# Hedgehog attention and spectral mix on one core: v loads on the software queue, permuted last sums with one store a pair, and a reordered tail

## The chip, the cores and the metric

The kernel runs on one core of one Trainium2 chip. The metric is the device time of one execution in microseconds (us), and the kernel before takes 462.76 us (median of three runs, 461.85 to 463.92).

The engines are called PE (matmul), PEld (its weight load), DVE (VectorE), ACT (ScalarE), POOL (GpSimd) and SP (SyncE). A DMA that SyncE issues goes to the hardware queue, q1 in the profile. One that GpSimd issues goes to the software queue, q0, and in this kernel all transfers that turn f32 into bf16 are issued there. The profile counts both queues against the same 16 DMA engines of the core. SBUF is the on-chip memory of 128 partitions that holds the tiles; PSUM is the one into which PE writes its sums.

## The reference

```python
batch, n_heads, seq, head_dim, d_feat = 8, 8, 576, 64, 128
def phi(x):                                   # x: q or k
    proj = einsum('bhsd,df->bhsf', x, w_phi)
    proj -= max(abs(proj), axis=-1)
    return concat([exp(proj), exp(-proj)], axis=-1)
num = q_p @ (k_p^T v);  den = q_p . sum_s(k_p) + 1e-6
x = (num / den) laid out as [8, 576, 512]     # attention output

X = rfft(x, axis=1)                           # 64 modes are used
Yr = Xr @ w_r[m] - Xi @ w_i[m]                # w_r, w_i: [64, 512, 512] f32
Yi = Xr @ w_i[m] + Xi @ w_r[m]
y = irfft(Y, n=576, axis=1)
u = x + y
return u + relu(u @ w_ch)                     # [8, 576, 512] f32, 9.44 MB
```

The two weight arrays are 134 MB of f32, so the kernel has to read 164 MB in all. That is most of its time.

## The kernel before

The work has three stages. In stage 1 attention runs and the weights stream in; each weight tile is read as f32 and lands as bf16. `mix` multiplies a tile with the spectrum. Eight modes make one group `o`, and a finished group is put into `yall` (for x) and, after a product with `w_ch`, into `zall` (for the relu argument). In stage 2, after the last weight tile, the last group goes through a chain: sum, transposes, copy, product, copy. In stage 3 the inverse transform of the last modes is added and the output is stored. The inverse transform of modes 0 to 47 is done earlier, in 36 "absorbs", one for each chunk of 128 rows; three of the 36 come in the last chain.

The loads (v has rows of 9 x 64 f32, which are 2304 bytes):

```python
def load(t, src, g, bp, eng):
    eng.dma_start(t.rearrange("p b c d -> p b (c d)"),
        src[2*bp:2*bp+2, 2*g:2*g+2].rearrange("b h (p c) d -> (h p) b (c d)", c=9))

def load_k(self): ...; load(self.kb, k, self.g, self.bp, pool)   # f32 -> bf16
def load_v(self): ...; load(self.vn, v, self.g, self.bp, sp)     # f32
```

The chain behind the last weight, with the absorbs in it:

```python
mix(*key, wts.pop(key), XTb[g % 2], bank)
...
dve.tensor_tensor(out=yst, in0=py, in1=yacc[:, o, :], op=ALU.add)
put(yst, o, yall, (0, 2))                # two small SyncE copies into yl
if end:
    ab[-3].sums(); ab[-3].keep_x()
for dc in range(4):
    pe.transpose(pt[:, dc, :], yst[:, dc*128:(dc+1)*128], ident_b)
act.copy(yT, pt)
if end:
    ab[-2].sums(); ab[-2].keep_x(); ab[-3].keep_w()
for dc in range(4):
    pe.matmul(pz, lhsT=yT[:, dc, :], rhs=wchb[:, dc, :], ...)
act.copy(zst, pz)
put(zst, o, zall, (1, 3))
if end:
    ab[-2].keep_w(); ab[-1].all()
```

The last sums. A chunk `n` has 128 rows: partition 64*a + p holds row 9*p + 4*a + c of a sequence, so the two halves `a` of the partitions go to two places of the output, and a pair of chunks is stored as two transfers of 64 partitions with 4 KB rows:

```python
class Last:
    def base(self, which):  # starts the PSUM sum: identity times the row so far
        ...
        pe.matmul(self.q[a], lhsT=ident_b, rhs=xw[:, self.bp, n, :], start=True, stop=False)
    def late(self, which): ...      # adds modes 48..63, table CL, from yl
    def straight(self, which): ...  # or the last group from yst / zst, table CM (first chunks)
    def relu(self): ...             # ACT: rl = relu(q)
    def store(self):
        ...
        dve.tensor_tensor(out=o, in0=self.pp, in1=self.rl, op=ALU.add)
        i, c = n // 4, n % 4
        for a in range(2):
            (sp, pool)[a].dma_start(
                rows[i][:, 4*a + c:4*a + c + 2, :], o[64*a:64*a + 64])   # 256 KB each
```

## Time and profile before

| | us, from the trace of the kernel before |
|---|---|
| stage 1: start to the last mix | 416.4 |
| stage 2: last mix to first store issued | 9.9 |
| stage 3: first store to end of the last DVE sum | 25.5 |
| end of the last sum to end of the span | 8.5 |
| span | 460.2 |

These lines are from the page of the kernel before: the DMA row gives the busy share of the 16 DMA engines in tenths, for 40 slices of 11.5 us; the GB/s row what they delivered; the queue lines give packets, MB, and the time of the packets as a share of the 16 engines' span; the last two give KB of one transfer and us from issue to landing.

```profile
span 460.2 us, 9716 instructions
...
DMA  8999999999999999999999999999999999992897
GB/s 192 207 216 220 230 229 209 228 229 207 229 230 209 228 229 227 209 230 229 207 229 228 207 207 207 206 208 207 207 213 218 214 211 211 205 178 55 249 323 252
DMA packets 86301, 99.27 MB, mean 216 GB/s; under 512 B 2800, under 2 KB 79728, under 8 KB 86256
...
q1 hardware_dynamic: 8992, 16.85, 12.0%
...
vn<-in_v_dram SPq DMA_DIRECT2D x16, 576.0 KB, 7.8
...
out_dram<-of SPq DMA_DIRECT2D x16, 256.0 KB, 4.9
```

The reader sees a full DMA row up to the 36th slice, then one slice at 55 GB/s, which is stage 2, then the output. A slice that carries weights alone shows 207 GB/s, because a weight is counted as the bf16 that lands; the f32 read is twice that, 414 GB/s.

This is the timeline of stage 2 in the kernel before: start us, duration, engine, operation, out<-in, count, and in brackets the idle time ahead of it and what ended that.

```profile
416.42 0.67 PE L37 MATMUL pt<-wt,XT 128*32 128x512 bf16 x8 [1.67 <-DMA wt<-in_moe_w_i_dram]
417.13 0.69 DVE L37 TENSOR_TENSOR yst<-pt,yacc 128x512 bf16<-128x512 f32 x1 [2.09 <-PE pt L37]
...
418.37 0.58 ACT L37 COPY yT<-pt 128x512 bf16<-128x512 bf16 x1 [2.94 <-PE pt L37]
...
419.01 1.04 PE L37 MATMUL pt<-wchb,yT 128*128 128x512 bf16 x3
...
420.13 0.58 ACT L37 CAST zst<-pt 128x512 bf16<-128x512 f32 x1 [0.68 <-ACT xw L37]
...
423.06 1.09 ACT L37 ACTIVATE rl<-qq 128x512 f32<-128x512 f32 x2 [1.37 <-PE qq L37]
...
425.01 1.23 DVE L37 TENSOR_TENSOR of<-pp,rl 128x1024 f32<-128x1024 f32 x1 [3.90 <-PE pp L37]
...
426.27 0.53 SPq L37 DMA_DIRECT2D out_dram<-of  x1
```

`zst` is ready at 420.71, yet its first use by the last sums is the matmul whose relu starts at 423.06, and the first output sum waits for the other half of its sum until 425.01. PE works on the remaining absorbs and on the base sums of a whole pair in between.

This is the table by stretch of time of the kernel before; its header line names the columns (busy us and count of each engine, the granted PE clock, the DMA share, GB/s).

```profile
core 0: us, PE busy (x) PEld busy (x) DVE busy (x) ACT busy (x) POOL busy (x), PEclk, DMA share, GB/s
416.00:426.00 10.00, 8.72 (x48) 3.09 (x48) 3.66 (x5) 4.55 (x9) 0.00 (x0) 1.00 0.22 54
428.00:444.00 16.00, 16.00 (x92) 4.81 (x88) 13.60 (x13) 11.56 (x21) 6.36 (x12) 1.00 0.95 312
444.00:452.00 8.00, 6.51 (x38) 1.94 (x36) 6.61 (x7) 4.94 (x9) 3.17 (x6) 1.00 0.94 305
452.00:458.00 6.00, 0.00 (x0) 0.00 (x0) 0.00 (x0) 0.00 (x0) 0.54 (x1) 0.62 0.95 310
```

In the output stage the DMA engines are 94 to 95% busy at only 305 to 312 GB/s, and after the last sum (452) they have six more microseconds of backlog. While v is being loaded the reading rate is also a bit lower: these are the queue lines of the DMA view of the kernel before from 251 to 253 us.

```profile
q1 hardware_dynamic: 174, 0.40, 57.3%
q0 software_dynamic: 173, 0.18, 51.4%
```

The weights' 0.18 MB are 0.36 MB of f32, so 0.76 MB are read in 2 us, 380 GB/s against the 414 of weights alone.

### The profile page before, as it was taken

What the parts mean: (1) busy time and instruction counts of PE and PEld (TensorE: products, weight loads), DVE (VectorE), ACT (ScalarE), POOL (GpSimd) and SP (SyncE); (2) the same over time, 40 slices, a digit from 0 to 9 for tenths busy, and PEclk for the clock granted to TensorE, in tenths of its full rate; (3) what the DMA queues carried; (4) which work ended last, traced back from release to release, by engine and by line L of the source; (5) the groups of instructions that cost most, each with busy time, mean ns of one, the idle gap of its engine ahead of it and who ended that gap; (6) DMA issues with size and microseconds to landing.
All of it is one profiled execution on the core that took longest, in us unless ns stands there. A gap on an engine that the chain in (4) does not pass through costs nothing.

```text
span 460.2 us, 9716 instructions
## 1 busy us (share of the span) xinstructions
PE 331.6 (72%) x4041; PEld 207.1 (45%) x4084; DVE 270.0 (59%) x488; ACT 281.6 (61%) x475; POOL 92.4 (20%) x130
## 2 busy tenths in 40 slices
PE   1586767768767767877866776059997756997991
PEld 1365546546555545655654554024443322332330
DVE  6656676556677658568647784643331213773882
ACT  3696879676889769579758762214452322664771
POOL 6232112113111211222110115002121210000331
PEclk9998999797999999789879999559998987999997
DMA  8999999999999999999999999999999999992897
GB/s 192 207 216 220 230 229 209 228 229 207 229 230 209 228 229 227 209 230 229 207 229 228 207 207 207 206 208 207 207 213 218 214 211 211 205 178 55 249 323 252
DMA packets 86301, 99.27 MB, mean 216 GB/s; under 512 B 2800, under 2 KB 79728, under 8 KB 86256
## 3 DMA queue, kind: packets, MB, share of 16 engines
q0 software_dynamic: 77264, 81.80, 103.8%
q1 hardware_dynamic: 8992, 16.85, 12.0%
q8 instruction: 32, 0.52, 0.4%
q14 instruction: 13, 0.11, 0.1%
HBM read 163.64 MB, written 9.44 MB: 376 GB/s over the span
## 4 chain that ended last, share of the span: by engine, by line
issue 27%; PE 23%; ACT 15%; DMA 15%; DVE 13%; POOL 5%; POOLq 0%; ACTq 0%
PE one L37 9%; PE pt L37 8%; DMA wt<-in_moe_w_i_dram 7%; PE two L37 6%; DVE m L37 6%; DMA kb<-in_k_dram 6%; ACT AB L37 5%; ACT AQ L37 5%; DVE mk L37 2%; POOL wt L37 2%; POOL out_dram L37 2%; DMA qb<-in_q_dram 2%; DVE zall L37 2%; ACT kT L37 2%; ACT XT L37 1%
## 5 line engine op out<-in xcount | busy, mean ns | idle before, releaser
L37 ACT CAST xw<-pt 128x512 bf16<-128x512 f32 x72 | 42.0, 586 | 61.7 <-PE pt L37 60.5
L37 ACT ACTIVATE AB<-two 128x1024 bf16<-128x1024 f32 x64 | 62.8, 1051 | 6.2 <-DVE mk L37 3.8
L37 ACT ACTIVATE AQ<-two 128x1024 bf16<-128x1024 f32 x64 | 63.0, 1053 | 1.9 <-PE two L37 1.8
L37 PE MATMUL pt<-wchb,xT 128*128 128x512 bf16 x135 | 39.8, 412 | 20.0 <-DVE xT L37 19.7
L37 DVE TENSOR_REDUCE m<-two 128x8 f32<-128x1024 f32 x32 | 39.2, 1224 | 17.8 <-PE two L37 17.7
L37 DVE TENSOR_REDUCE mk<-two 128x8 f32<-128x1024 f32 x32 | 39.0, 1221 | 16.7 <-PE two L37 16.3
L37 POOL DMA_DIRECT2D wt<-in_moe_w_r_dram x30 | 26.3, 878 | 95.7 <-PE one L37 52.9
L37 POOL DMA_DIRECT2D wt<-in_moe_w_i_dram x28 | 24.5, 876 | 91.0 <-PE pt L37 46.1
L37 DVE TENSOR_TENSOR va<-vn,ee 128x1152 bf16<-128x1152 f32 x32 | 42.0, 1356 | 0.0
L37 DVE RECIPROCAL rd<-one 128x6 f32<-128x6 f32 x48 | 9.4, 195 | 51.5 <-PE one L37 51.5
L37 ACT COPY kT<-one 128x512 bf16<-128x512 bf16 (+1 forms) x32 | 19.2, 640 | 28.7 <-PE one L37 28.7
L37 DVE TENSOR_TENSOR xs<-pt,xs 128x512 bf16<-128x512 f32 x36 | 24.3, 691 | 19.0 <-PE pt L37 18.6
L37 PEld LDWEIGHTS <-minus 96*128 96x128 bf16 x288 | 26.3, 110 | 19.0 <-issue 13.4
L37 PEld LDWEIGHTS <-XT 128*32 128x32 bf16 x512 | 17.9, 180 | 34.2 <-issue 21.6
L37 PE MATMUL two<-w2blk,qT 128*128 128x256 bf16 x128 | 20.4, 285 | 17.6 <-ACT AB L37 12.9
L37 DVE COPY xT<-pt 128x512 bf16<-128x512 bf16 x36 | 15.1, 422 | 30.3 <-PE pt L37 30.3
L37 PE MATMUL two<-mT,minus 96*128 96x128 bf16 x256 | 29.3, 245 | 3.1 <-issue 1.9
L37 PEld LDWEIGHTS <-xs 128*128 128x128 bf16 x304 | 24.7, 100 | 15.2 <-issue 8.1
L37 POOL DMA_DIRECT2D kb<-in_k_dram x16 | 11.5, 716 | 95.5 <-PE one L37 94.7
L37 PEld LDWEIGHTS <-qT 128*128 128x128 bf16 x144 | 14.1, 101 | 32.5 <-issue 29.9
L37 PE MATMUL one<-kvz,AQ 128*128 128x65 bf16 x512 | 28.0, 211 | 0.0
L37 DVE TENSOR_TENSOR xs<-one,rd 128x384 bf16<-128x384 f32 x48 | 26.8, 558 | 1.6
(113 smaller groups left out, 673.9 us busy)
## 6 DMA issues: line engine op xcount, KB each, us to landing
wt<-in_moe_w_r_dram POOLq DMA_DIRECT2D x30, 1024.0 KB, 28.1
wt<-in_moe_w_i_dram POOLq DMA_DIRECT2D x28, 1024.0 KB, 28.6
vn<-in_v_dram SPq DMA_DIRECT2D x16, 576.0 KB, 7.8
kb<-in_k_dram POOLq DMA_DIRECT2D x16, 288.0 KB, 22.3
qb<-in_q_dram POOLq DMA_DIRECT2D x16, 288.0 KB, 22.1
out_dram<-of SPq DMA_DIRECT2D x16, 256.0 KB, 4.9
out_dram<-of POOLq DMA_DIRECT2D x16, 256.0 KB, 5.0
xs<-in_moe_w_i_dram POOLq DMA_DIRECT2D x2, 1024.0 KB, 26.9
```

What stands on the lines that cost most here:

```text
L37: ins = f(*args, **kwargs)
```

## The change

There are three intents. The v loads go to the software queue, with all other large loads. The output pairs are to be stored by one transfer over all 128 partitions: a permutation matrix takes the identity's place in the last sums and the tables' columns are permuted alike, so that partition 2*p + a holds what partition 64*a + p held. And the tail is reordered: all 36 absorbs come ahead of the last mix; the products of the last three chunks are held in PSUM; the sum, the transposes, the copies and the product of the last group are split into halves of 256 columns, and of the copies ACT takes one half and DVE the other; and the first pair is split into two single chunks, of which the first has its sums started ahead of the last term. The diff also joins the stores of the ninth rows of two batch pairs into one, puts half of the last small copies into `yl` on GpSimd's queue, and drops the separate PSUM pools of the last sums. `K` is 33, so `ab[K:]` are the last three chunks.

```diff
-            load(self.vn, v, self.g, self.bp, sp)
+            load(self.vn, v, self.g, self.bp, pool)
...
+    perm = CF.rearrange("p c r m -> p (c r m)")[:, 512:640]
+    dve.tensor_copy(perm.rearrange("k (p a) -> k a p", a=2),
+                    ident_b.rearrange("k (a p) -> k a p", a=2))
...  (the columns of CL and CM are written in the same order)
+        def hold(self, pf):          # product of a chunk, left open in PSUM
+            for g in range(NG):
+                pe.matmul(pf, lhsT=self.xT[:, g, :], rhs=wchb[:, g, :],
+                          start=(g == 0), stop=False)
...
-    todo += [c.all for c in ab[:-3]]
+    todo += [c.only_x for c in ab[K:]] + [c.only_w for c in ab[K:]] + [c.all for c in ab[:K]]
...
+        if not mixq:                 # ahead of the last mix
+            seq[0].base(1)
+            seq[0].late(1)
         mix(*key, wts.pop(key), XTb[g % 2], bank)
...
+            if end:
+                seq[0].base(0)
+                seq[0].late(0)
...  (yst, yT, zst in two halves of 256 columns; of the copies to yT and zst one half on ACT, one on DVE)
-            if end:
-                ab[-3].sums()
-                ab[-3].keep_x()
...  (likewise ab[-2], ab[-1])
+            elif end:
+                seq[0].straight(0)
+                seq[0].keep_p()
+                seq[1].base(1)
...
+                turned = perm if n < 8 else ident_b
-            for a in range(2):
-                (sp, pool)[a].dma_start(
-                    rows[i][:, 4 * a + c:4 * a + c + 2, :], o[64 * a:64 * a + 64])
+            sp.dma_start(
+                bass.AP(tensor=rows.tensor, offset=rows.offset + n % 4 * DMODEL,
+                        ap=[[9 * DMODEL, 64], [4 * DMODEL, 2], [1, w * DMODEL]]),
+                o.rearrange("p a e -> p (a e)") if w > 1 else o)
...
+    seq = [Last((0, 0)), Last((0, 1))] + [Last(*x) for x in pairs[0][1:] + pairs[1]]
+    seq += [Last((0, 8), (1, 8))] + [Last(*x) for x in pairs[2]] + [Last((2, 8), (3, 8))]
+    seq += [Last(*x) for x in pairs[3]]
```

## The prediction

> **What bounds it now.** Three stages follow one another. (1) Up to 416 us, weight loading. The DMA row is full from 5 to 410 us; the software queue delivers 207 GB/s of bf16, so reads 413 GB/s of f32 (page and per-queue window view). The last mix starts at 416.42, after 1.67 us of waiting for its weight (timeline); PE's absorbs had just fitted. (2) 416.4 to 426.3: a latency chain (sum 0.69, transposes 0.40, copy 0.58, product 1.04, copy 0.58 us) with three absorbs in its way, then the first output pair; DMA share 0.4 (stage table). (3) Output: 9.44 MB from 426.3 to 459. The first output sum starts at 425.0, the last ends at 451.7; PE needs 1.29 us a pair, DVE 1.28. The DMA share is 0.9 to 1.0 at only 300 to 350 GB/s, SyncE's late issues are stretched to 1.7 us, and stores are issued until 455: the DMA is the limit there, compute close behind.
>
> **Costs.** *v on the software queue*: the same bytes. The Trainium skill (DMA: Bandwidth & Descriptors, Issuing engines are not separate DMA queues) says that all issuers share 16 engines, so no bandwidth by itself. But while v flows, the two queues' packets make up 370 to 390 GB/s of reading, against 413 otherwise (1 us windows, 250 to 253): 0.2 to 0.25 us lost a load, 16 loads, at most 4 us. I credit 1.5 us. v lands after about 25 us instead of 7.8, against some 30 us of lead: it just fits, with rare DVE waits that DMA backlog hides.
> *Reordering*: three absorbs (2 us of PE) leave the final chain, three held products fill the idle PE at 377 to 384, halves shorten the chain, and the first chunk needs only its last term. I estimate the first store 4.6 us after the last weight, instead of 9.85: 5 us, all on the critical path. Chunk four's sums then wait shortly (0 to 1 us) for the last small copies (3.4 us landing before). After that 16 steps at about 1.3 us: last store about 30 us after the weight, against 35.3 for the last DVE sum (and 38.5 for SyncE's last issue) before.
> *Stores*: 40 become 19, so completion packets go from 640 to 304. Stores used 466 engine-us; at 25.8 GB/s an engine (the loads' rate) data is 366, leaving 0.156 us a completion packet. Estimate after: 413 engine-us, 25.8 us instead of 29.1, so the stores keep up nearly. The skill (SBUF, Door 1) says that 64 partitions reach half the ports, about 218 GB/s; this trace shows 290 GB/s from SyncE's 64-partition stores alone (456 to 457), so I count little for the full 128. One queue is enough: SyncE issues in 0.6 us when not pushed back.
>
> **Sum.** 462.8 less 1.5 (v), 5.2 (first store), about 3 (drain after compute: 8.5 us becomes 5.5) = 453.0 us; range 449 to 457.5. Chances: faster 0.54, same 0.45, slower 0.01.
>
> **What would show it.** Last mix at 414 to 416.5 us; first store within 5 us of it; DVE output sums 1.3 us apart; under-512 B packets down by 336; output at 360 to 400 GB/s; last store issue near 445; span near 450.5. The v step is right if reading stays above 405 GB/s while v flows; wrong if DVE waits on v leave the DMA row with holes.
>
> **What would make it wrong.** Stores on one queue stuck at 320 to 330 GB/s (455 or more); v late enough to starve the weights; PE, now with 36 absorbs before the last mix and only four single banks, reaching it after the weight; or, to the good, an evener finish of the 16 engines, whose rates fell off unevenly from 410 to 416 (up to 3 us), or v recovering all 4 us.

## The result, and the profile after

The changed kernel takes 452.34 us (median of four runs, 451.45 to 452.55), against 462.54 of four runs of the kernel before. The ratio is 0.9772 (95% interval 0.9745 to 0.9799), so it is faster by 2.3%. A ratio here and below is the mean time of one kernel's runs over that of the other's in the same rounds, so it is not quite the ratio of the medians that are quoted. The kernel before ran on the same chip, so kernels are compared by these ratios.

The two traces add up as follows. Each row is one stage, and the last column is what the changed kernel gains in it.

| us | before | after | gained |
|---|---|---|---|
| last mix starts | 416.42 | 414.26 | 2.16 |
| last mix to first store | 9.85 | 5.15 | 4.70 |
| first store to end of the last sum | 25.45 | 26.32 | -0.87 |
| end of the last sum to end of span | 8.48 | 4.67 | 3.81 |
| span | 460.2 | 450.4 | 9.8 |

This is one profile of each. In the repeat after_again the four stages are 413.25, 5.17, 26.31 and 4.77 us, so the first row is uncertain by about 1 us, and the others repeat within 0.1.

These are the lines of the page of the changed kernel that answer to those shown above, with the group of DVE that reads v (busy us, mean ns, then idle time ahead of it and what ended that).

```profile
span 450.4 us, 9754 instructions
...
DMA  8999999999999999999999999999999999995597
GB/s 162 233 207 207 234 208 234 232 208 261 207 207 234 234 234 232 213 230 227 217 230 225 229 218 206 206 207 207 209 207 220 214 215 214 202 201 100 195 380 314
DMA packets 83981, 99.27 MB, mean 220 GB/s; under 512 B 2464, under 2 KB 79136, under 8 KB 83936
...
q1 hardware_dynamic: 5744, 11.86, 8.1%
...
L37 DVE TENSOR_TENSOR va<-vn,ee 128x1152 bf16<-128x1152 f32 x32 | 42.0, 1355 | 3.4 <-DMA vn<-in_v_dram 3.4
...
vn<-in_v_dram POOLq DMA_DIRECT2D x16, 576.0 KB, 18.4
out_dram<-of SPq DMA_DIRECT2D x17, 512.0 KB, 3.6
```

A v load now takes 18.4 us to land instead of 7.8, and DVE waited for v for 3.4 us in all. The DMA row has no hole while v flows, so those waits cost nothing (v_first2_sp below agrees). Packets under 512 B fell by 336, as predicted. A store of 512 KB lands in 3.6 us, where one of 256 KB took 4.9.

The timeline of the changed kernel, from the last mix to the first store, with the columns of before:

```profile
414.26 0.67 PE L37 MATMUL pt<-wt,XT 128*32 128x512 bf16 x8 [1.43 <-DMA wt<-in_moe_w_i_dram]
...
414.98 0.76 DVE L37 TENSOR_TENSOR yst<-pt,yacc 128x256 bf16<-128x256 f32 x2 [2.25 <-PE pt L37]
...
416.34 1.04 PE L37 MATMUL pt<-wchb,yT 128*128 128x256 bf16 x8
...
417.20 0.37 ACT L37 CAST zst<-pt 128x256 bf16<-128x256 f32 x1 [0.28 <-PE pt L37]
...
418.69 0.69 DVE L37 SCALAR_TENSOR_TENSOR ofr<-pp,rl 128x512 f32<-128x512 f32 x1 [0.80 <-PE pp L37]
...
419.41 0.61 SPq L37 DMA_DIRECT2D out_dram<-ofr  x1
```

The product starts 2.08 us after the last mix (2.59 before), the first output sum 4.43 us after it (8.59 before). `zst` is whole 3.64 us after it (its DVE half ends at 417.90), against 4.29 before. So of the 4.70 us by which the first store comes earlier, 0.65 are gained up to `zst`, 3.51 between `zst` and the first output sum, where the sums of a single chunk now stand ready and no absorb is in the way, and 0.54 in an output sum of half the size. This is read from the two traces; no run took the halves or the split of the first pair away alone. The table by stretch of the changed kernel, with the columns of before:

```profile
414.00:419.00 5.00, 4.68 (x30) 2.19 (x31) 1.78 (x5) 1.33 (x3) 1.05 (x2) 1.00 0.21 52
...
428.00:444.00 16.00, 15.86 (x99) 4.98 (x97) 13.85 (x12) 12.36 (x24) 0.00 (x0) 1.00 0.95 372
444.00:448.00 4.00, 0.25 (x2) 0.00 (x0) 1.72 (x2) 0.47 (x1) 0.00 (x0) 0.89 1.02 406
```

The same busy share of the DMA engines, 0.95, now carries 372 GB/s instead of 312, and 406 from 444 us on, as the last sums end. PE is busy for nearly all of 428 to 444 in both kernels.

### The profile page after: what moved, and what is told of

It reads as the page before. It is cut to its first block, busy times and chain, and to the rows that moved or that the text cites. A ratio compares the mean times of both kernels' runs of the same rounds, so it can differ in the third digit from the quotient of the medians.

```text
span 450.4 us, 9754 instructions
## 1 busy us (share of the span) xinstructions
PE 329.1 (73%) x4069; PEld 209.5 (47%) x4113; DVE 276.3 (61%) x519; ACT 274.6 (61%) x472; POOL 94.8 (21%) x128
## 3 DMA queue, kind: packets, MB, share of 16 engines
HBM read 163.64 MB, written 9.44 MB: 384 GB/s over the span
## 4 chain that ended last, share of the span: by engine, by line
DMA 28%; PE 26%; issue 17%; ACT 12%; DVE 12%; POOL 5%; ACTq 0%; POOLq 0%; DVEq 0%
DMA wt<-in_moe_w_i_dram 13%; PE pt L37 11%; PE one L37 8%; DMA wt<-in_moe_w_r_dram 8%; DMA vn<-in_v_dram 6%; ACT AB L37 5%; PE two L37 4%; DVE m L37 3%; POOL wt L37 3%; ACT AQ L37 3%; PE pp L37 3%; DVE mk L37 2%; DVE zall L37 2%; DVE va L37 1%; DVE xs L37 1%
## 5 line engine op out<-in xcount | busy, mean ns | idle before, releaser
L37 ACT CAST xw<-pt 128x512 bf16<-128x512 f32 x50 | 29.4, 588 | 43.2 <-PE pt L37 43.2
L37 PE MATMUL pt<-wchb,xT 128*128 128x512 bf16 x127 | 36.3, 398 | 22.4 <-DVE xT L37 20.8
L37 PE MATMUL two<-w2blk,qT 128*128 128x256 bf16 x128 | 21.9, 299 | 16.5 <-ACT AB L37 12.3
L37 PEld LDWEIGHTS <-xT 128*128 128x128 bf16 x144 | 13.4, 102 | 32.0 <-DVE xT L37 20.5
L37 PE MATMUL pt<-wt,XT 128*32 128x512 bf16 x208 | 18.5, 431 | 11.4 <-DMA wt<-in_moe_w_i_dram 8.7
L37 PE MATMUL one<-kvz,AQ 128*128 128x65 bf16 x512 | 26.6, 206 | 0.1
## 6 DMA issues: line engine op xcount, KB each, us to landing
vn<-in_v_dram POOLq DMA_DIRECT2D x16, 576.0 KB, 18.4
```

What stands on the lines that cost most here:

```text
L37: ins = f(*args, **kwargs)
```

## The experiments

Twelve kernels ran; ten of them compute the right result. The questions were three. Why do the v loads gain more than the 1.5 us that the prediction gave them? Is the faster output due to fewer completion packets (called C1), as the prediction had it, or to the 128 partitions of a transfer, that is to more ports of SBUF (C2)? And does the reordering gain its time by taking the absorbs out of the chain? A run's first store and last sum are times in its trace.

| kernel | median us (range, runs) | ratio to before | first store | last sum ends | span |
|---|---|---|---|---|---|
| v_only | 458.46 (458.21-458.94, 6) | 0.9938 | 423.35 | 448.80 | 456.5 |
| no_v | 454.28 (453.67-455.12, 4) | 0.9846 | 422.84 | 449.15 | 453.3 |
| split_halves | 460.45 (457.47-463.16, 6) | 0.9981 | 421.58 | 451.16 | 461.4 |
| no_reorder | 455.61 (455.34-456.00, 4) | 0.9875 | 423.38 | 448.98 | 454.2 |
| absorbs_early | 463.46 (460.53-464.78, 6) | 1.0032 | 427.58 | 453.04 | 460.9 |
| split_cols | 454.61 (453.73-458.65, 6) | 0.9867 | 418.99 | 445.30 | 451.9 |
| after_again | 451.98 (451.33-452.27, 4) | 0.9782 | 418.42 | 444.73 | 449.5 |
| halves_warm | 457.88 (457.09-459.46, 6) | 0.9917 | 418.35 | 444.67 | 455.5 |
| absorbs_warm | 461.46 (460.59-461.86, 5) | 0.9988 | 426.30 | 451.75 | 459.7 |
| v_first2_sp | 451.62 (451.42-452.93, 5) | 0.9784 | 418.42 | 444.72 | 449.8 |

The kernel before had medians of 461.23, 461.49 and 461.78 us in the three calls (11 runs each). The 95% intervals of the ratios are within 0.0034 of them. The two kernels that compute nothing, micro_stores and micro_loads, ran once each and are read by their traces alone.

### v_only: the kernel before with v on the software queue

```diff
-            load(self.vn, v, self.g, self.bp, sp)
+            load(self.vn, v, self.g, self.bp, pool)
```

> The kernel before with nothing changed but the 16 loads of v, which go to the software queue. Theory A (v travels faster there, because that queue packs two 2304-byte rows in a packet and so the reads keep near 410 GB/s): last mix about 2 us earlier than the 416.42 of before (414 to 415), time 1.5 to 2.5 us lower, 460 to 461 us. Rival B (the earlier last weight of the changed kernel comes from its reordering, not from v): last mix at 416 to 417, time within 0.5 us of before.

It takes 458.46 us, ratio 0.9938 (0.9924 to 0.9951), which is 2.8 us. The last mix starts at 413.49 instead of 416.42, 2.9 us earlier, and the stretches from there to the first store (9.86 us) and to the last sum (25.45 us) have their old lengths; the end behind the last sum is 0.8 us shorter in this one profile. So the one word is worth about twice what the prediction credited, and it comes in stage 1. By 285 us, when all of v has landed, 62.89 MB have been delivered against 62.41 in the kernel before; at the 207 GB/s of the weights, the 0.48 MB are 2.3 of the 2.9 us.

These are the last mix in v_only and, for the next run, in no_v:

```profile
413.49 0.67 PE L37 MATMUL pt<-wt,XT 128*32 128x512 bf16 x8 [1.67 <-DMA wt<-in_moe_w_i_dram]
417.68 0.67 PE L37 MATMUL pt<-wt,XT 128*32 128x512 bf16 x8 [0.97 <-DMA wt<-in_moe_w_i_dram]
```

### no_v: the changed kernel with v back on SyncE

```diff
-            load(self.vn, v, self.g, self.bp, pool)
+            load(self.vn, v, self.g, self.bp, sp)
```

> The changed kernel with v back on SyncE's queue. Theory A: last mix back at about 416.4, everything after it shifted whole, 2 us slower than the changed kernel, 454 to 455 us. Rival B: last mix stays near 414.3, 452.3 us.

It takes 454.28 us, ratio 0.9846 (0.9830 to 0.9863), against 0.9772 of the full change and 0.9782 of its repeat: 3.4 or 3.0 us by the ratios. The last mix starts at 417.68, 3.42 us later than in the changed kernel. This agrees with v_only. It also starts 1.26 us later than in the kernel before, which loads v the same way. That would suggest that the reordering delays the last mix, but it is not shown: the six profiled kernels that have the new order and at least 14 of the 16 v loads on the software queue start it anywhere from 413.18 to 414.58, and the old order with v there starts it at 413.49 (v_only) and 413.51 (no_reorder).

### split_halves: the changed kernel with two 64-partition stores a pair

```diff
-            sp.dma_start( ... all 128 partitions ... )
+            for h in range(2):
+                (sp, pool)[h].dma_start(
+                    bass.AP(tensor=rows.tensor,
+                            offset=rows.offset + n % 4 * DMODEL + 32 * h * 9 * DMODEL,
+                            ap=[[9 * DMODEL, 32], [4 * DMODEL, 2], [1, w * DMODEL]]),
+                    src[64 * h:64 * h + 64])
```

> The changed kernel, permuted rows kept, but each pair stored as two 64-partition transfers of 256 KB, one from SyncE and one from GpSimd, as before the change. Theory C (the number of transfers, or the half of the partitions in each, sets the output rate): output back at 310 to 345 GB/s, last sum unchanged near 446 or pushed by at most 1 us, drain 7 to 8.5 us instead of 4.7, 3 to 4 us slower than the changed kernel, 455 to 456.5. Rival D (the order of addresses that the permutation gives, or simply the earlier start, does it): 452 to 453 us and rates of 370 to 400 GB/s.

It takes 460.45 us, with a wide range of 457.47 to 463.16, ratio 0.9981 (0.9950 to 1.0011): nearly the whole gain is gone, which is more than either theory expected. The output moves 290 GB/s from 428 to 444 us with the rows permuted, so rival D, the order of addresses, is out. Its profile is of its slowest run, and one line of the table by stretch shows a second thing that happened in it, besides the stores (columns as above; 0.57 is the granted PE clock):

```profile
416.00:424.00 8.00, 7.99 (x28) 2.79 (x27) 2.16 (x5) 2.33 (x5) 2.20 (x4) 0.57 0.39 98
```

PE ran at half clock while the first chunks were due. The run therefore mixes two effects, and halves_warm below separates them.

### no_reorder: the kernel before with v on the software queue and one store a pair

The edit is v_only plus the permutation matrix, the permuted tables, and the wide store of the change; the order of everything else is the old one.

> The kernel before with v on the software queue and with permuted rows and one SyncE transfer a pair, but its own order of absorbs and first chunks. If the parts add: v 2 us and the shorter drain; the first store still 9.85 us after the last weight. The drain should shrink to about 4 to 5 us after the last sum (8.5 before), so 462.6 - 2 - 3.8 = 456.5 to 457 us if stores catch up, and the reordering's share is the remaining 4 to 5 us. If the shorter drain depends on the earlier start, the gain here is 2 to 3 us only (460).

It takes 455.61 us, ratio 0.9875 (0.9859 to 0.9890), a little better than expected. Against v_only the wide stores gain 0.63%, 2.9 us; the reordering, on top of that, gains another 0.9 to 1.0%, 4.3 to 4.7 us. This line of the DMA view is from 428 to 444 us:

```profile
DMA packets 1704, 5.69 MB, mean 356 GB/s; under 512 B 191, under 2 KB 191, under 8 KB 1702
```

### micro_stores: eight ways to store 8.39 MB

This kernel gives a wrong result. It stores constant tiles to the output, in eight phases with a DVE write between them, so that the phases do not overlap.

```python
PAIRS = [(bp, n) for bp in range(NP) for n in (0, 2, 4, 6)]    # 16 pairs of 512 KB
def halves(queues, rows_of):   # two transfers of 64 partitions, 4 KB rows
    for bp, n in PAIRS:
        for a in range(2):
            h = rows_of(a)
            queues[a].dma_start(rows[:, 4*a + c:4*a + c + 2, :], o[h:h + 64])
def whole(queues, cut): ...    # cut = 1: one transfer of 128 partitions, 4 KB rows;
                               # cut = 2: two of 128 partitions, 2 KB rows
```

> Only stores, no compute (wrong result on purpose: constants). One zeroed tile of 128 x 1024 f32 is stored over 8.39 MB of the output eight times, each phase waiting for the one before: 1: 64-partition halves of 256 KB from SyncE and GpSimd, as before the change; 2: 512 KB over 128 partitions from SyncE, as after; 3: the halves both from SyncE; 4: 128 partitions in two column halves of 256 KB (2 KB rows), SyncE; 5: 64-partition halves, all from partitions 0 to 63, SyncE; 6: as 2, by turns from SyncE and GpSimd; 7: as 4, by turns; 8: as 2, GpSimd. Theory C1 (completion packets: 0.156 us each of an engine): phases 1, 3, 5 all at 330 to 345 GB/s, 2, 6, 8 at 375 to 385, 4 and 7 at or below phase 1. Theory C2 (64 partitions reach half the ports of the memory): phase 5 near 218 GB/s, 1 and 3 between, 2, 4, 6, 7, 8 all at 390 to 410.

| phase | us for 8.39 MB | GB/s when steady |
|---|---|---|
| 1: halves, SyncE and GpSimd (as before) | 31.0 | 303 |
| 2: whole, SyncE (as after) | 22.8 | 406 |
| 3: both halves on SyncE | 33.4 | 272 |
| 4: whole in two column halves, SyncE | 24.1 | 381 |
| 5: 64 partitions, always 0 to 63, SyncE | 42.95 | 210 |
| 6: whole, SyncE and GpSimd in turn | 24.0 | 399 |
| 7: column halves, SyncE and GpSimd in turn | 26.1 | 368 |
| 8: whole, GpSimd | 24.3 | 388 |

The lines of the table by stretch for phases 1 to 5 and 7 (here DVE and POOL alone have busy columns; then the PE clock, the DMA share and GB/s):

```profile
10.00:30.00 20.00, 0.00 (x0) 2.87 (x6) 1.00 1.01 303
36.00:54.00 18.00, 0.00 (x0) 0.00 (x0) 1.00 1.02 406
60.00:88.00 28.00, 0.00 (x0) 0.00 (x0) 1.00 0.81 272
94.00:113.00 19.00, 0.00 (x0) 0.00 (x0) 1.00 1.02 381
120.00:156.00 36.00, 0.00 (x0) 0.00 (x0) 1.00 0.97 210
...
190.00:208.00 18.00, 0.00 (x0) 5.82 (x10) 1.00 1.02 368
```

This settles C1 against C2 as the main cause. Phase 4 has twice the transfers of phase 2, hence twice the completion packets, and shorter rows as well, and costs 1.27 us for 16 x 16 more completion packets on 16 engines: at most 0.079 us of an engine for each, where the prediction had estimated 0.156 from C1. On two queues, phase 7 costs 2.02 us more than phase 6, at most 0.126 us for each. Phase 3 has the transfers and the queue of phase 4, but each covers 64 partitions, and costs 9.3 us more; on two queues, phase 1 costs 4.9 us more than phase 7. So the 8.15 us from phase 1 (as before) to phase 2 (as after) are 4.9 for the partitions, 2.0 for fewer transfers with longer rows and 1.2 for one queue instead of two. C2 is not the whole either: it expected 390 to 410 GB/s of phases 4, 7 and 8, and they reached 381, 368 and 388. Phase 5 shows a 64-partition transfer bare: 210 GB/s at a DMA share of 0.97, so the busy share does not fall when the engines move only half as much. The Trainium skill (SBUF — State Buffer, Door 1: The DMA port swizzle) says that partitions 0 to 63 reach 8 of 16 ports, with an asymptote of about 218 GB/s; this run agrees, at 210. The 218 in the expectation is that figure. The prediction quoted that and set it aside, because of one microsecond of the trace that read 290 GB/s. That window, at the very end of the kernel before, was no measurement of a steady rate (0.04 MB of GpSimd's stores ran in it beside the 0.29); why it showed 290 stays open.

### split_cols: the changed kernel with two 128-partition stores a pair

```diff
+            c = w * DMODEL // 2
+            for h in range(2):
+                (sp, pool)[h].dma_start(
+                    bass.AP(..., offset=rows.offset + n % 4 * DMODEL + h * c,
+                            ap=[[9 * DMODEL, 64], [4 * DMODEL, 2], [1, c]]),
+                    src[:, h * c:h * c + c])
```

> The changed kernel with each pair stored by two transfers of 256 KB again (SyncE and GpSimd), but both over all 128 partitions (2 KB rows). Theory C1 (number of transfers): as slow as the 64-partition split or slower, 455 to 457 us. Theory C2 (partitions in a transfer): like the changed kernel, 452 to 453 us.

It takes 454.61 us (453.73 to 458.65), ratio 0.9867 (0.9835 to 0.9900), between the two theories. It has about as many transfers as split_halves, on the same two queues, but each reaches all partitions, and from 428 to 444 us it moves as much as the changed kernel does (a line of the DMA view):

```profile
DMA packets 2621, 5.96 MB, mean 372 GB/s; under 512 B 335, under 2 KB 335, under 8 KB 2618
```

It is 1.1% faster than split_halves, whose profile shows a lost PE clock besides, and 0.5% (2.3 us) faster than halves_warm below, whose profile shows none. Its best run is 2.3 us slower than the best of the changed kernel, near the 3.3 us that phase 7 takes over phase 2, and 3.4 us faster than the best of halves_warm. By the means it is 0.9 to 1.0% (3.9 to 4.4 us) slower than the changed kernel, because three of its six runs lie 1.3 us and more above the other three; only the fastest was profiled, and what slowed those is open. So in the kernel, too, both count: the partitions, and fewer transfers with longer rows on one queue. That the partitions are the larger part is shown by micro_stores, and here by the best runs alone.

### micro_loads: seven ways to read v and weights

This kernel, too, is wrong: it only loads, v in its 16 transfers and weights in their tiles.

```python
p = ['only_v(sp)', 'only_v(pool)', 'only_v(sp, True)',       # True: rows of 4608 B
     'only_w(16)', 'both(sp)', 'both(pool)', 'both(sp, True)']
```

> Only loads (wrong result on purpose: constants). Phases of 16 loads each: 1: v alone from SyncE (2304-byte rows); 2: v alone from GpSimd; 3: v alone from SyncE with 4608-byte rows; 4: weights alone from GpSimd, cast to bf16; 5: v from SyncE beside weights; 6: v and weights both from GpSimd; 7: as 5 with 4608-byte rows of v. Theory A1 (packet size): phase 1 reads at 340 to 375 GB/s, phases 2 and 3 at 400 to 411, 4 at 413; 5 in the stretch with both at 370 to 390 of reading, 6 and 7 at 405 or more. Rival A2 (two queues by turns cost time): phases 1, 2, 3 alike, 5 and 7 both at 370 to 390, 6 at 410.

Alone, v is read at 392 GB/s by SyncE (2304-byte rows), 391 by the software queue and 413 by SyncE with 4608-byte rows. So the software queue is no faster by itself; that expectation missed. Neither theory holds as a whole: A2 fits phases 1, 2, 5 and 6, but not phases 3 and 7. Weights alone deliver 207 GB/s and read 414. The queue lines of the DMA view for v on SyncE beside weights (82 to 120 us):

```profile
q1 hardware_dynamic: 3513, 7.62, 58.3%
q0 software_dynamic: 3509, 3.54, 54.7%
```

This is 7.62 + 2 x 3.54 = 14.70 MB read in 38 us, 387 GB/s, the same loss that the kernel before shows. With both on the software queue (275 to 340 us):

```profile
q0 software_dynamic: 11920, 16.47, 119.8%
```

Here 36% of the MB delivered are v, so 27.0 MB are read in 65 us, 415 GB/s. With 4608-byte rows on SyncE beside the weights it is 402 in a short stretch of 17 us. (The DVE writes did not hold back the next phase's v loads fully, so weights alone and v beside weights overlap somewhat; the windows lie inside the clean stretches.)

What follows: while v flows, v and weights on two queues are read 7% slower than on one queue. The two windows do not hold the same mix, though: v is 52% of the MB read in the first and 22% in the second. At the rates that each reaches alone such mixes would be read at 402 and 409 GB/s by calculation, so about a quarter of the difference can be the mix, and the rest is the two queues. All v (9.44 MB) with the weights that go with it in the first window is 18.2 MB, which takes 47.0 us at 387 GB/s, 45.3 at 402 and 43.9 at 415: 1.8 to 3.2 us by this calculation, and 2.8 to 3.4 were measured. The Trainium skill (DMA: Bandwidth & Descriptors, Issuing engines are not separate DMA queues) says that issuing from several engines only saves the sequencer's time; for these two queues the runs show otherwise.

One candidate for the reason is the packets: the software queue packs two v rows into one packet. Up to 285 us the kernel before has 55858 - 51762 = 4096 packets between 2 and 8 KB, one for each of the 16 x 256 rows of v; the changed one has 54364 - 52316 = 2048. But the packing by itself is not it: alone, the software queue reads v at 391 GB/s in 1188 packets for 5.47 MB, and SyncE at 392 in 2724 for 6.28 MB. Rows of 4608 B on SyncE read 413 alone and 402 beside weights, so two queues lose some 3% with long rows, too, where the mix loses nothing. That the engines take turns between the two queues would explain it, but no run shows it; the cause of the loss is not settled.

### absorbs_early: the kernel before with all absorbs ahead of the last mix

```diff
-    todo += [c.all for c in ab[:-3]]
+    todo += [c.all for c in ab]
...  (the three absorbs behind `if end:` are deleted)
```

> The kernel before with all 36 absorbs ahead of the last mix, none left in the chain after it. First chunks, halves, stores and v stay as before. If the three absorbs cost what they hold on PE: chain from weight to first store shorter by about 2 us (9.85 to about 7.9), PE reaching the last mix up to 0.5 us after the weight; 460.5 to 461.5 us. If nothing: the chain's waits on the copies were the limit and absorbs sat in its gaps.

It takes 463.46 us, ratio 1.0032 (1.0005 to 1.0059): 0.3% slower, not faster. The last mix starts at 415.96, without a wait for its weight, and the first store comes at 427.58, later than before, although the chain has less work. The table by stretch of the profiled run shows why, in the chain:

```profile
418.00:424.00 6.00, 4.77 (x12) 1.36 (x13) 0.00 (x0) 1.76 (x4) 0.00 (x0) 0.55 0.36 87
```

The granted clock is 0.55: without the absorbs PE idles, and its matmuls then take about twice as long (the product of the chain 1.88 us instead of 1.04). The Trainium skill (TensorE: Matmul & The Clock Gate, Part 1) says that PE falls to half clock after an idle window of about 3.4 us, that the window runs freely, and that the result varies from run to run. The trace agrees in the half clock (0.50 from 420 to 424 us). It shows no idle gap of that length: PE's longest gap between the last mix and the fall was 0.80 us here, and 1.40 us, just ahead of the last mix, in split_halves, while the changed kernel kept 1.00 after a gap of 1.43 us. Whether the clock varies between runs of one kernel is not shown, as absorbs_early and split_halves were profiled once each.

### absorbs_warm: the same with dummy matmuls in the gaps

```diff
+    def warm(n):
+        b = bank()
+        for _ in range(n):
+            pe.matmul(b, lhsT=ident_b, rhs=wchb[:, 0, :], start=True, stop=True)
...  (warm(2) ahead of the transposes, ahead of the product, and after zst)
```

> The kernel before with all absorbs ahead of the last mix, with six matmuls into an unread bank in the gaps of the last chain. Theory E (the early absorbs did shorten the chain, but the empty PE then dropped to half clock): with the gaps filled the clock stays at 1.0 and the time comes to 460 to 461, up to 1.5 us below before and 2 to 3 us below the unfilled version. Rival F (the absorbs sat in the chain's gaps and cost nothing): filled or not, no better than before.

The clock stays at 1.00 in the same stretch:

```profile
418.00:424.00 6.00, 5.20 (x28) 1.75 (x24) 0.69 (x1) 2.28 (x5) 0.00 (x0) 1.00 0.31 77
```

It takes 461.46 us, ratio 0.9988 (0.9967 to 1.0009): the same as the kernel before. The chain from the last mix to the first store is 8.85 us instead of 9.85, so 1.0 us is gained, but the last mix starts at 417.45, 1.03 us later and without any wait for its weight: PE worked on the absorbs without a gap up to it. (In absorbs_early, which has the same order up to there, it started at 415.96, so the 1.03 us is the figure of one profile.) Moving the absorbs alone gains nothing that the times show; in this profile the work only moves from behind the weight to ahead of it.

The changed kernel may avoid this because it starts earlier on them. It puts the held products and the first absorb parts into a stretch where PE of the kernel before was idle. Before, PE was busy for 1.60 of the 7 us from 377 to 384, and its clock was 0.50 in the four microseconds after; in the changed kernel it was busy for 5.65 of the 7 us from 372 to 379 and its clock stayed at 1.00. This part is read from the two traces; no run took it away alone.

### halves_warm: split_halves with four dummy matmuls ahead of the last mix

```diff
             seq[0].late(1)
+            warm(4)
         mix(*key, wts.pop(key), XTb[g % 2], bank)
```

> The 64-partition split again, with four matmuls into an unread bank while PE waits for the last weight, so that PE's clock does not fall. If its 457.5 to 463.2 us of before was the clock's doing in part, the runs close up to 456 to 458 and the profile shows the clock at 1.0 from 414 to 424; the rest against the changed kernel (4 to 6 us) is then the cost of the 64-partition stores. If not the clock, it stays spread around 460.

It takes 457.88 us (457.09 to 459.46), ratio 0.9917 (0.9894 to 0.9940), so with PE kept warm, 0.6% of the time that split_halves had lost comes back. The profile has the clock at 1.00 now:

```profile
416.00:424.00 8.00, 8.00 (x42) 2.56 (x41) 4.19 (x5) 4.23 (x8) 2.16 (x4) 1.00 0.57 144
```

The rest of the loss is the stores. The first store (418.35) and the end of the last sum (444.67) are as early as in the changed kernel (418.42 and 444.73 in after_again), and the whole loss comes behind them: the span ends 10.8 us after the last sum instead of 4.8. Two more lines by stretch of the same kernel:

```profile
428.00:444.00 16.00, 15.05 (x92) 4.69 (x90) 13.92 (x12) 11.94 (x22) 5.03 (x10) 1.00 0.99 321
444.00:453.00 9.00, 0.00 (x0) 0.00 (x0) 0.66 (x1) 0.00 (x0) 0.89 (x2) 0.54 0.97 291
```

The DMA share is 0.97 to 0.99 at 291 to 321 GB/s. From 428 us on the output is limited by the stores, and an earlier start of the sums only makes the backlog at the end longer.

### after_again and v_first2_sp

The first is the changed kernel once more. The second asks whether the 3.4 us of DVE waits on v cost anything: it puts the first two v loads back on SyncE.

```diff
-            load(self.vn, v, self.g, self.bp, pool)
+            load(self.vn, v, self.g, self.bp, sp if self.g == 0 and self.bp < 2 else pool)
```

> The changed kernel unchanged, for its spread. If dips of PE's clock after the last weight strike at random, some of these runs should be 2 to 5 us over the rest; if the changed kernel's fuller chain is safe from them, all runs stay within 1 us of 452 (as four did).

> The changed kernel with the first two loads of v put back on SyncE, where they start at 2 us while the software queue is still filling; the other fourteen stay on the software queue. If the idle DMA of the first 5 us can be used: 0.3 to 1.0 us faster than the changed kernel, 451.3 to 452. If only the two loads' lower rate counts: 0.4 us slower.

The changed kernel repeats at 451.98 us, ratio 0.9782 (0.9760 to 0.9805); its eight runs lie between 451.3 and 452.6. v_first2_sp takes 451.62, ratio 0.9784 (0.9760 to 0.9807): no difference, so its expectation missed. DVE waited for v for 2.0 us in it and for 6.2 us in after_again, so those waits cost nothing; the DMA backlog covers them, as the prediction had said. No run beat the changed kernel.

### Stores and order together

The four kernels with v on the software queue make a table of two by two, in ratios to the kernel before:

| | stores in halves | one wide store | wide gains |
|---|---|---|---|
| old order | 0.9938 | 0.9875 | 0.6%, 2.9 us |
| new order, PE warm | 0.9917 | 0.9772 / 0.9782 | 1.4%, 6.2 to 6.7 us |
| new order gains | 0.2%, about 1 us | 0.9 to 1.0%, 4.3 to 4.7 us | |

Each part gains more beside the other. With half stores the DMA is the limit of stage 3, and starting earlier gains 1 us. With wide stores in the old order the sums are the limit (356 GB/s at a DMA share of 0.90 from 428 to 444 in no_reorder), and faster stores only shorten the end. (The halves of v_only hold unpermuted rows, those of halves_warm permuted ones, so the table is not quite one factor at a time.)

## Why the prediction was right

The time (453.0 predicted, 452.34 measured) and the class were right, and the structure held: three stages in a row, and a gain in each of the three places named. The terms of the sum were less exact, and their errors offset each other.

- *v credited with 1.5 us.* Mis-sized. v_only and no_v show 2.8 to 3.4 us (in the profile of the changed kernel the last mix came only 2.16 us earlier, in that of its repeat 3.17). The prediction had the right measure of it (370 to 390 GB/s of reading while v flows, at most 4 us) but credited less than half of it without a reason from the trace. Its sign of success, reading above 405 GB/s while v flows, is what micro_loads shows for one queue: 415.
- *First store 5 us earlier after the weight.* 4.7 us measured (9.85 to 5.15); 4.6 us from weight to store were predicted. The size is right. Of its reasons, "three absorbs (2 us of PE) leave the final chain" is not a gain by itself: absorbs_warm gains 1.0 us in the chain, and its time is the same (0.9988). The two traces put 3.51 of the 4.70 us behind `zst`, where the first chunk lacks only its last term, as the prediction had it; no run tested that part alone.
- *16 steps of about 1.3 us, last store about 30 us after the weight.* The last sum ended 31.5 us after it, so this stage is 0.87 us longer than before and about 1.5 us longer than predicted.
- *Drain 8.5 us becomes 5.5.* It became 4.67. The gain is right and its reason is not. "I count little for the full 128" is the step that failed: micro_stores shows that the partitions of a transfer are the main thing (303 against 406 GB/s with two halves or one whole), and that a completion packet costs at most 0.079 us on one queue and 0.126 on two, not the 0.156 that the prediction worked out. The prediction arrived at nearly the right rate (9.44 MB in 25.8 us are 366 GB/s, and 372 was measured) with the wrong main cause: by its own reason, stores of 64 partitions, halved in number, would have done as well, and phase 5 with its 210 GB/s speaks against that (no run stored so in the kernel).
- *Signs in the profile.* Last mix at 414 to 416.5: 414.26. First store within 5 us: 5.15. Packets under 512 B down by 336: exactly. Output at 360 to 400 GB/s: 372, then 406. Last store issue near 445: 445.7. Span near 450.5: 450.4.

Taken together, by the two profiles: stage 1 gave 2.16 us where 1.5 were credited, the first store 4.70 where 5.2 were, the later sums took 0.87 where nothing was, and the drain gave 3.81 where 3 were. That is 9.80 us against 9.7. The four errors cancel, so this closeness is partly luck. (Of the 0.66 us by which the median lies below 453.0, 0.26 is that the four runs of the kernel before have a lower median than the 462.8 that the prediction began with.)

What stays open: why two queues read v and weights more slowly; why PE kept its clock in both profiles of the changed kernel, whose eight runs agree within 1.3 us, although split_halves, with the same instructions up to the first stores, lost it in its one profile; what each part of the reordering gives; and whether the reordering delays the last mix.

## What to carry to other kernels

Let a store cover all 128 partitions, even if a permutation has to be put into a matmul that is there anyway: that was worth more than fewer transfers, and a DMA row that is 95% busy does not tell whether it moves 312 or 372 GB/s. When two parts of a change act on the same stage, one that starts the work earlier and one that drains it faster, test them in a table of two by two, because each may be worth little alone. When work is taken out of a latency chain, look at where it goes and whether PE keeps its clock without it.

## What the Trainium skill lacked or had wrong

- DMA: Bandwidth & Descriptors, Issuing engines are not separate DMA queues: issuing from several engines is said to save only the sequencer's time, and no cost is named. Here v on SyncE beside weights on GpSimd read 387 GB/s, and both on GpSimd 415; in the kernel the move of v to one queue is worth 2.8 to 3.4 us.
- No page was found to say when GpSimd's queue puts two rows of 2304 B into one packet, where SyncE's has a packet for each row: 4096 packets between 2 and 8 KB against 2048 for the same 16 loads.
- SBUF — State Buffer, "Can I just issue two DMAs to hit both halves?": two concurrent halves are said to gain 6% over one. Here halves of both sides reached 272 GB/s from one queue and 303 from two, against 210 from partitions 0 to 63 alone, which is 30 and 44% more. One transfer over 128 partitions is still better (406).
- No page was found to say how long the tail is with which a stream of loads ends: in the kernel before the delivered rate fell from 181 GB/s to 33, microsecond by microsecond, from 410 to 416 us, at the end of the weights.
